# Projection weights of a mixture-of-experts layer: one transfer over 128 rows for each kind instead of two over 64

## The chip, the core and the metric

The kernel runs on one core of a Trainium2 chip. The core has a matrix engine (TensorE: PE for its matmuls, PEld for its weight loads), three engines that work on rows of elements (VectorE or DVE, ScalarE or ACT, GpSimd or POOL), a synchronisation engine SP that here only issues transfers, and 16 DMA engines that carry them between DRAM and the on-chip memory. Each engine runs its own list of instructions in order. An instruction waits on semaphores for what it reads, and what stands behind it on the same engine waits with it. The metric is the time of one execution on the device in microseconds, as a median of several.

## What is computed

The first half is a linear attention with a norm, the second a layer of four experts, each of them a causal attention with its own projections, of which each token uses two:

```python
kv = einsum('bhsd,bhse->bhde', k, v)          # b, h, s, d = 8, 8, 576, 64
out = einsum('bhsd,bhde->bhse', q, kv)
out = out / sqrt(mean(out * out, -1) + 1e-06) * g_norm
x = out.transpose(0, 2, 1, 3).reshape(8, 576, 512)
logits = x @ w_gate                            # 4 experts, the two best are used
for e in range(4):
    q, k, v = x @ wq[e], x @ wk[e], x @ wv[e]  # 512 x 64 each
    a = softmax(causal(q @ k.T / 8))
    y += weight_of_expert(e) * (a @ v @ wo[e])
```

All inputs and the output are float32.

## The kernel before

Each of the eight batches goes through the same steps, and several batches are under way at once. Per batch: load k, v and q (L360 to L379); the products of k and v (`kv`, L382, on TensorE at L387), which are copied out of the accumulator memory as `kvs` (L392) and, with neighbouring rows exchanged, as `kvx` (`kv_move`, L395); 32x32 transposes of q on VectorE (L401); `out_mm` (L408, matmuls at L414), which reads qT, kvs and kvx; copies of its result to `o_sb`; sums of squares and gate logits (L443); a spread of the norm factors over the rows (L562) and the scaled, transposed activations `xT` (L573). Then the experts, two at a time: `proj` (L599, matmuls at L602) makes kT and qT of a pair of experts, `v_mm` (L584, L587) the values of all four; scores (L620), exponentials (L631), masks (L637), the product with the values (L649), scaling (L669), a transposition (L682), and the output product (L694) with its store (L715).

The norm's gain `g_norm` and a constant are folded into the projection weights. Row d of head h in a weight is multiplied by element d of the gain, so a weight is loaded unscaled into a staging area (`lw`, L338) and then copied with the factor into its final tile `w_r` (`ws`, L344). The staging area is the memory of the three tiles `PT`: PT_143 for q, PT_144 for k, PT_145 for v. The final tile `w_r[kind]` has 128 rows (which of two groups of four heads, times 64 elements), four chunks (the head within the group), four experts and 64 columns.

Before, a transfer `lw(kind, eh)` brings two of the four experts in full, 512 rows each, into 64 rows of the staging area: 256 KB as 64 x 16 runs of 256 bytes. A scaling `ws(kind, hh, eh)` takes four heads of two experts out of those 64 rows and writes one half of the rows of `w_r`, all four chunks, for two experts. So one transfer and the two scalings that follow it complete two experts. The projections of batch 0 begin with experts 2 and 3 (pair 1), and experts 0 and 1 (pair 0) follow after `out_mm` of batch 1.

All instructions stand in one list that was written out ahead of time, as three strings: `ORDER` gives the tasks in order, `ENGINE` the engine of each task, `BANKS` the banks of the accumulator memory. A task's instructions go to its engine in the order of that list. A fourth string, `GATE`, limits the loads in flight: the digit n at a load's place makes it wait until the load that is n places earlier in the list of loads has landed (0: no such wait). SP issues the loads in that order, so a load that waits holds back the loads behind it.

Names in rows of the order: k_b_80, v_b_82 and q_b_84 are the buffers of k, v and q of batch 1 (batches use two buffers of each in turn), k_b_79, v_b_81 and q_b_83 those of batches 0 and 2; kvs_86 and kvx_88 are the products of batch 1; xT_133 is the activation of batch 0; kT_136 and qTp_139 are the projections of its pair 1.

Of the kernel before, what the change touches and what calls it, by code (L numbers as in the profile page):

```python
# [24 lines left out]


ORDER = (
    "010A0v0t0D060714130N0P0Q0R050C0U0u0r0s0z020J0S040803000w0x152w0E160I0-"
    "0y0+101112170L1A191C2x180M091E1L1G1H1F2t1D1B1M1N1O0Y0i2u1P1Q1K1R340h2v0W1g1i1I1j1h1J2y2+1k1l0B0d2-"
    "302z31333235362H0e2F0X0f0g0V0c2G372I0b0F383A3B4w393G3H1u1s3C3D2N3E3F4y2O3J1v1S1T1U0O2P1V3K1t1+3L1-"  # L30
    "4x4v513M522Q501X4-"
    "53541W203N4z56574+591w1x583O0Z0a21552J3I3T2K0l0T0m5A0j5E6z6y0k5B5C5G1q1r3P3Q3R1o6x3S3i5F2U1p5H5I1Z3l8+5D1m6+0K"
    "1n3k3j5K3n5J5L3m3U3V5M5N3W1Y5O5P2L1y3X5Q5R5S6-2M8-"
    "3Y1z2R3w3x71735T2T72743Z753a5U782S5l775o3u3b3v5p765V4J4K5k5W5n4H5m90703s42797B3y7A4I8z3+953-"
    "3t229243459693941b1a1c1d970G3z0p7C7GA-"
    "7D9C919A9BB22V99B12W1e1f7E7K7L9D2X98235y5z5w5x7H7I2Y253q3rB30n3d3o9E443p9F7J7F9G249I9M9K622Z63262728290o472A2B"
    "2C2D5s5tB02a2b2cBC4L4M7N9L0q5XD53c3e4R0HBD7O7P7Q5Z407R7S4S2E4W4T7T7U7V416061B7B8B5B6B964657W4N4O9H9J6L6M6J6K7m"
    "D17oD25Y9N9P7p7n9Q7r5u5v7q3f9R9S9T2d2k2l4U2h3gB44648495aBF3h2i4A4C4D4E2e2f5dD39U4F2n2o4B4P4Q4V5+2p679O9ZD47M7X"
    "5-5e6T6UBB6N6O5bBE6R7+7-"
    "4X4Y4Z4a4b4c9V9W4d4e9XBA6S6X5c9Y8L8M5q5r692gBGBH7YBIF8F3BKBO5fBJ5g5hBM6Y2jBN7Z7b8N9p8O9t2m9s7y7z7u6P5i7vD6F682"  # L40
    "8485DH835j6Q2q2r4GDE6VD9BL684f6WDAD87aD79o894jBPF7DB4m9q664g9rDD4h6d6eDG6f7w9+7x6g4n6A2sDCF46Z6a6b4k9-"
    "86878T6E8U4o9w9x6B6C6DF5A0A16cDF6F6G6H6I7dDIDKDM7c7e9a7f9b9cDJDQDO8ABRBSFH8BBQ8VFG7gBTBUBV4iDL7h7i8PDP8W8aBWA6"
    "7j8Q8081A7BbBXBY9u9vDR4p4q7s7t6hA84rA4BZBa8R4sA57k4lA9FCDN8S7l4tFBFAFI9d9e9f9gF9FDFF6u6vBrBvBu8XDT4uBqBs6w6l88"
    "DUDV6m6nBt8G6oDWDX8ZFE6r6s6p6i8C8DFJ8E8HC29hC08I6qDY6j6kC38F8J8Y6t8f8gC19y9z8K9i8hBc8b8c8dBd8iBwBx8eFKFOBeDZFL"
    "FMFSB+B-"
    "FQ8jBfC69jCAADDa9kFTC8DbC7DcC9FR9l9mACANAOCBAPAQDtDwDxDSDdFPDeFNBgBjAVAWAbA2A3AXAY8w8x8yAA8k8lCRCSAcDsDvDuFVFW"
    "FXFYFZFUFaBkABFfATAUARASC4C5AEAFAIFbBhCPCQ9nETCEAG8n8oAJAKAa8mALAHAMFcFdEUAZAdCZFgCaCXCYCVCTAeAfAgAhAi8pAjDfAk"
    "Al8q8rDgDhCdCUE2E3CFCCBiCW8t8uE4E5FeBlBmCcByBzDjFuFw8sE6E7BnBoDyDzAsApFxFvFyDiCe8vFzAtDlAyAzA+ERAvAwAmAnEAAqCb"
    "DkAuESArEVEZCDCGEBAxDnCHBpCICJCKDmEWCLCMCNG4G5EGAoCfCgChCOCjCkEaEfCiD+ClFhG2CmG3EbFiD-EdFjCnFkEXEcFlE8ECEYEDG6"
    "E9GWE0FnGXFoG7GEGFEHEeGCDoDpDqE1G8G9FmFpFqFrDrEEEFGAGBEgGUEIEJG0GDEKELG1GIGVEMENElEOEhEmEnEPEQGeGfGcGdGjGiGHGa"  # L50
    "GbGGEoGYGhEiEjEkEpGJF+F-CuC+C-D0FsFtCvCwCoGZGKGLGMCrGNCsGOGPGgGkGlGQGRCxCtCpCqCyCzGmGnEzE+GoGpGqGrE-"
    "EqEwErEsGSGTGsEtExEyEuF0GtH4H5G+EvF1F2H1H6G-H0H2GuGvGxGwGyGzH3"
)
# [65 lines left out]
def kernel(  # L119
# [125 lines left out]
    def queue(*task):  # L245
        return {"S": nc.sync, "A": nc.scalar, "G": nc.gpsimd}[engine[task]]
# [88 lines left out]
        nc.vector.tensor_reduce(m_b[:], jj[:, :, 2], axis=AX_X, op=add)  # L335
        nc.vector.tensor_scalar(out=m_b[:], in0=m_b[:], scalar1=-1.0, scalar2=None, op0=mult)

    def lw(nm, eh):  # L338
        return queue("lw", nm, eh).dma_start(
            stage[nm][eh * Dh : (eh + 1) * Dh].rearrange("p e h f -> p (e h) f"),  # L340
            w_dram[nm][2 * eh : 2 * eh + 2].rearrange("e (h p) f -> p (e h) f", p=Dh),
        )

    def ws(nm, hh, eh):  # L344
        rows = slice(eh * Dh, (eh + 1) * Dh)
        src = stage[nm][rows, :, 4 * hh : 4 * hh + 4, :]
        dst = w_r[nm][hh * Dh : (hh + 1) * Dh, :, 2 * eh : 2 * eh + 2, :].rearrange("p c e f -> p e c f")
        if engine["ws", nm, hh, eh] == "A":
            nc.scalar.activation(dst, src, ACTF.Copy, scale=g8[rows, 0:1])
        else:  # L350
            ew("ws", nm, hh, eh).tensor_scalar(out=dst, in0=src, scalar1=g8[rows, 0:1], scalar2=None, op0=mult)
# [428 lines left out]
```

## Time and profile before

| | |
|---|---|
| time, median of 3 runs | 208.63 us (208.28 to 209.16) |
| profiled execution, own time | 208.9 us |
| its span in the trace | 206.9 us |
| busy: PE, DVE, ACT, POOL | 185.5, 140.8, 125.9, 77.1 us |
| mean share of the DMA engines, 35 to 41 us | 1.09 |
| projection (L602): matmuls for the key and query weights | 20.6 and 20.8 us in all |
| weight scalings on POOL, 64x512 elements | 1.56, 1.56 and 1.84 us |
| weight scalings on ACT, 64x512 elements | 0.72 us each, six |

The profile shows one execution on the chip. Its views are: a page with the busy time of each engine, the chain of work that ended last, the costliest groups of instructions and the transfers; instructions in order of time (start, duration, engine, line, operation, output from input, and in brackets how long the engine sat idle before and what ended that); busy time by window; and the transfers that were issued in a window, with the time from issue to landing. A "q" behind an engine's name is its instruction queue, so SPq rows are issues of transfers. A clock of 1.00 is the full clock of TensorE. A DMA share above 1 means that packets overlap on the 16 engines.

### The profile page before, as it was taken

What the parts mean: (1) busy time and instruction counts of PE and PEld (TensorE: products, weight loads), DVE (VectorE), ACT (ScalarE), POOL (GpSimd) and SP (SyncE); (2) the same over time, 40 slices, a digit from 0 to 9 for tenths busy, and PEclk for the clock granted to TensorE, in tenths of its full rate; (3) what the DMA queues carried; (4) which work ended last, traced back from release to release, by engine and by line L of the source; (5) the groups of instructions that cost most, each with busy time, mean ns of one, the idle gap of its engine ahead of it and who ended that gap; (6) DMA issues with size and microseconds to landing.
All of it is one profiled execution on the core that took longest, in us unless ns stands there. A gap on an engine that the chain in (4) does not pass through costs nothing.

```text
span 206.9 us, 7270 instructions
## 1 busy us (share of the span) xinstructions
PE 185.5 (90%) x3009; PEld 146.3 (71%) x3020; DVE 140.8 (68%) x359; ACT 125.9 (61%) x216; POOL 77.1 (37%) x187
## 2 busy tenths in 40 slices
...
GB/s 210 361 228 296 268 197 190 367 249 314 351 352 314 329 230 284 49 290 205 219 266 308 277 188 117 97 71 221 37 3 81 82 136 55 205 37 24 159 354 217
DMA packets 41905, 42.62 MB, mean 206 GB/s; under 512 B 17936, under 2 KB 35344, under 8 KB 41872
## 3 DMA queue, kind: packets, MB, share of 16 engines
...
q10 hardware_dynamic: 2208, 1.84, 2.7%
...
## 4 chain that ended last, share of the span: by engine, by line
PE 69%; DMA 10%; DVE 7%; issue 5%; ACT 2%; POOL 2%; DVEq 0%; SPq 0%; POOLq 0%; ACTq 0%
PE ps L602 15%; PE ps L387 8%; PE ps L443 8%; PE ps L587 8%; PE ps L620 8%; PE ps L649 7%; PE ps L414 7%; PE ps L694 7%; DMA k_b<-in_k_dram 6%; DMA OT<-osc 3%; DVE qT L403 2%; DMA q_b<-in_q_dram 2%; DVE kvx L229 2%; PE ps L562 1%; ACT PT L631 1%
## 5 line engine op out<-in xcount | busy, mean ns | idle before, releaser
L631 ACT ACTIVATE PT<-ps 128x1024 bf16<-128x1024 f32 (+1 forms) x64 | 50.7, 837 | 11.7 <-PE ps L620 8.9
L637 POOL TENSOR_SCALAR_AFFINE_SELECT PT<-PT 128x256 bf16<-128x256 bf16 (+1 forms) x80 | 29.2, 389 | 25.2 <-ACT PT L631 24.9
L403 DVE STREAM_TRANSPOSE qT<-q_b 128x576 f32<-128x576 f32 x32 | 23.6, 759 | 13.7 <-DMA q_b<-in_q_dram 11.8
L387 PE MATMUL ps<-v_b,k_b 128*64 128x64 f32 x640 | 22.3, 234 | 6.5 <-DMA k_b<-in_k_dram 5.8
L573 DVE TENSOR_TENSOR xT<-o_sb,ps 128x640 fp32r<-128x640 f32 x30 | 23.4, 814 | 6.3 <-PE ps L562 5.0
L387 PEld LDWEIGHTS ps<-v_b,k_b 128*64 128x64 f32 x640 | 21.4, 149 | 8.5 <-issue 6.2
L587 PE MATMUL ps<-wv_r,xT 128*128 128x256 f32 x160 | 23.6, 289 | 0.4 <-DVE root L474 0.4
L436 POOL TENSOR_TENSOR sq<-o_sb 128x576 f32<-128x576 f32 x16 | 18.4, 1159 | 10.6 <-ACT o_sb L226 7.0
L587 PEld LDWEIGHTS ps<-wv_r,xT 128*128 128x128 f32 x160 | 20.3, 189 | 2.5 <-issue 0.7
L620 PE MATMUL ps<-qTp,kT 64*128 64x64 f32 (+4 forms) x192 | 21.3, 338 | 0.0
L602 PE MATMUL ps<-xT,wq_r 128*128 128x288 f32 x128 | 20.8, 304 | 0.0
L602 PE MATMUL ps<-xT,wk_r 128*128 128x288 f32 x128 | 20.6, 304 | 0.2 <-ACT PT L631 0.2
L602 PEld LDWEIGHTS ps<-xT,wk_r 128*128 128x128 f32 x128 | 17.6, 188 | 2.3 <-issue 0.7
L649 PEld LDWEIGHTS <-PT 128*128 128x128 bf16 x480 | 16.3, 97 | 3.7 <-issue 1.0
L694 PE MATMUL ps<-wo_b,OT 128*128 128x512 bf16 (+1 forms) x85 | 18.1, 344 | 0.8 <-DMA OT<-osc 0.4
L602 PEld LDWEIGHTS ps<-xT,wq_r 128*128 128x128 f32 x128 | 17.6, 188 | 1.3 <-issue 0.4
L649 PE MATMUL ps<-vext,PT 128*128 128x65 bf16 x480 | 18.1, 193 | 0.1
L620 PEld LDWEIGHTS ps<-qTp,kT 64*128 64x128 f32 x192 | 14.0, 185 | 5.3 <-issue 1.4
L669 DVE TENSOR_TENSOR osc<-ps,inv 128x384 bf16<-128x384 f32 (+1 forms) x32 | 15.2, 485 | 2.6 <-POOL inv L665 2.0
L226 ACT COPY o_sb<-ps 128x576 f32<-128x576 f32 x19 | 11.6, 643 | 6.9 <-PE ps L414 6.9
L229 DVE COPY o_sb<-ps 128x576 f32<-128x576 f32 x13 | 9.8, 756 | 8.4 <-PE ps L414 5.6
L414 PE MATMUL ps<-qT,kvs 32*64 32x288 f32 x256 | 13.5, 415 | 1.4 <-issue 0.9
...
## 6 DMA issues: line engine op xcount, KB each, us to landing
...
out_dram<-y SPq DMA_DIRECT2D x24, 256.0 KB, 2.5
...
out_dram<-v_b SPq DMA_DIRECT2D x4, 256.0 KB, 3.6
...
```

Source lines behind the costliest of these rows:

```text
L387: nc.tensor.matmul(p_kv[Dh * t : Dh * t + Dh, j, hh, :], lhsT=kb_[b % NK][:, h, n, :], rhs=vb_[b % NK][:, h, n, :], start=(n == 0), stop=( ...
L403: nc.vector.transpose(qT_[0][:, hh, j * n : (j + 1) * n].rearrange("p j h i -> p (j h i)"), qb_[b % 2][:, hh, j * n : (j + 1) * n, :].rear ...
L414: nc.tensor.matmul(p_o[Dh * hh : Dh * hh + Dh, 0:HALF], lhsT=kvx_[b % 2][rows, hh, :] if m else kvs_[b % 2][rows, g % 2, hh, :], rhs=qT_[0 ...
L436: inst = ew("sq", b, u, p).tensor_tensor(out=dst, in0=src, in1=src, op=mult)
L573: ew("xm", b, u, p).tensor_tensor(out=view(xT_[b % 2]), in0=view(ob_[b % 2]), in1=spread_r.rearrange("p s (m j) -> p m s j", j=32), op=mult)
L587: nc.tensor.matmul(one("v", b, i)[:, n * 256 : (n + 1) * 256], lhsT=xT_[b % 2][:, c, blk * P : (blk + 1) * P], rhs=w_r["v"][:, c].rearrang ...
L602: nc.tensor.matmul(bank_in((nm + "p", b, pr), s)[:, 0:HALF], lhsT=w_r[nm][:, c, 2 * pr : 2 * pr + 2, :].rearrange("p e f -> p (e f)"), rhs ...
L620: nc.tensor.matmul(bank_in(("sc", b, pr, j), el)[:, o : o + hi - lo], lhsT=kT_[(2 * b + pr) % 3][pp, kb * P : (kb + 1) * P], rhs=qTp_[(2 * ...
L631: nc.scalar.activation(PT[:, :, d0 : d0 + o], two("sc", b, pr, j)[:, :, 0:o], ACTF.Exp, scale=scale)
L637: nc.gpsimd.affine_select(out=d, in_=d, compare_op=AluOpType.is_ge, fill=0.0, base=0, pattern=[[0, 2], [1, w]], channel_multiplier=-1)
L649: nc.tensor.matmul(p_O[:, (2 * n + el) * (Hd + 1) : (2 * n + el + 1) * (Hd + 1)], lhsT=PT[:, el, col : col + P], rhs=vx_[b % 2][:, kb, 2 * ...
L694: nc.tensor.matmul(p_y[o * nq : (o + 1) * nq, 0:w], lhsT=OT_[b % 2][:, pr, s0 : s0 + nq], rhs=wo_b[:, pr, o * w : (o + 1) * w], start=(pr ...
```

## The change

A weight's transfer now takes all four experts at once over 128 rows, with row = 64 x (parity of the head) + element, so 512 KB as 128 x 16 runs of 256 bytes. There is one transfer for each of the three kinds in place of two. Since a staging row now holds four heads of one parity for all experts, a scaling `ws(kind, hh, x)` reads two heads of one parity x for four experts, and writes one half of the rows of `w_r`, every second chunk, for all four experts. There are still four scalings of each kind, on the same engines.

```diff
-    out += [("lw", nm, eh) for nm in "qkv" for eh in r2] + [("ws", nm, hh, eh) for nm in "qkv" for eh in r2 for hh in r2]
+    out += [("lw", nm) for nm in "qkv"] + [("ws", nm, hh, x) for nm in "qkv" for x in r2 for hh in r2]
...
-        nm: PT_[n][:].rearrange("p e n -> p (e n)")[:, 0 : 2 * D * E * Hd // P].bitcast(FP32).rearrange("p (e h f) -> p e h f", e=2, h=H)
+        nm: PT_[n][:].rearrange("p e n -> p (e n)")[:, 0 : 2 * D * E * Hd // P].bitcast(FP32).rearrange("p (e n f) -> p e n f", e=E, n=NCH)
...
-    def lw(nm, eh):
-        return queue("lw", nm, eh).dma_start(
-            stage[nm][eh * Dh : (eh + 1) * Dh].rearrange("p e h f -> p (e h) f"),
-            w_dram[nm][2 * eh : 2 * eh + 2].rearrange("e (h p) f -> p (e h) f", p=Dh),
-        )
-
-    def ws(nm, hh, eh):
-        rows = slice(eh * Dh, (eh + 1) * Dh)
-        src = stage[nm][rows, :, 4 * hh : 4 * hh + 4, :]
-        dst = w_r[nm][hh * Dh : (hh + 1) * Dh, :, 2 * eh : 2 * eh + 2, :].rearrange("p c e f -> p e c f")
+    def lw(nm):
+        return queue("lw", nm).dma_start(
+            stage[nm].rearrange("p e n f -> p (e n) f"), w_dram[nm].rearrange("e (n p) f -> p (e n) f", p=P)
+        )
+
+    def ws(nm, hh, x):
+        rows = slice(x * Dh, (x + 1) * Dh)
+        src = stage[nm][rows, :, 2 * hh : 2 * hh + 2, :]
+        dst = w_r[nm][hh * Dh : (hh + 1) * Dh, x : x + 3 : 2, :, :].rearrange("p n e f -> p e n f")
...
-    "000000065544044055564506006553456430300023036240420420606"
+    "000000065544044556450606553456430300023036240420420606"
```

The last pair is `GATE`. Its digits for the dropped loads are gone and most of the others are as before, but they count back in a list that is three entries shorter, so ten of the other loads wait for another load than before. The first v load of batch 2 waited for the last k load of batch 1 and now waits for the k weights. `ORDER` places the k scalings on POOL and ACT and three of the q scalings ahead of the first projection. `BANKS` gives another bank number to 81 of 282 results in the accumulator memory. The line numbers of the changed kernel are one higher from L29 to L338.

On SP, around the loads of batch 1 (`-` before, `+` now):

```order
 L363 DMA k_b_80<-in_k_dram 64x8x320
-L339 DMA PT_144<-in_moe_wk_dram 64x16x64
+L340 DMA PT_144<-in_moe_wk_dram 128x16x64
 L363 DMA v_b_82<-in_v_dram 64x8x320
 L363 DMA k_b_80<-in_k_dram 64x8x256
-L339 DMA PT_143<-in_moe_wq_dram 64x16x64
+L340 DMA PT_143<-in_moe_wq_dram 128x16x64
 L376 DMA q_b_84<-in_q_dram 128x1152
-L339 DMA PT_144<-in_moe_wk_dram 64x16x64
-L339 DMA PT_143<-in_moe_wq_dram 64x16x64
 L363 DMA v_b_81<-in_v_dram 64x8x320
 L363 DMA v_b_81<-in_v_dram 64x8x256
```

The whole k weights stand where their first half stood, ahead of the last v and k loads of batch 1; the whole q weights likewise behind them. The second halves are gone from behind the q load.

On TensorE, the end of `kv` of batch 1 (L387), the first two projections (L602) and the first of `out_mm` of batch 1 (L414), with what each instruction waits for. A name such as Pool_49 is the semaphore that counts POOL's finished instructions, Activation_49 that of ACT. Before:

```order
L387 MATMUL ps<-v_b_82,k_b_80 64x64 x31
L602 MATMUL ps<-xT_133,wk_r 128x288 [waits DVE_49,Pool_49]
L602 MATMUL ps<-xT_133,wk_r 128x288 x3
L602 MATMUL ps<-xT_133,wk_r 128x288 [waits Pool_49]
L602 MATMUL ps<-xT_133,wk_r 128x288 x3
L602 MATMUL ps<-xT_133,wq_r 128x288 [waits Activation_49]
L602 MATMUL ps<-xT_133,wq_r 128x288 x7
L414 MATMUL ps<-qT_89,kvs_86 64x288 [waits DVE_49] x2
```

And with the change:

```order
L387 MATMUL ps<-v_b_82,k_b_80 64x64 x31
L602 MATMUL ps<-xT_133,wk_r 128x288 [waits DVE_49,Activation_49,Pool_49]
L602 MATMUL ps<-xT_133,wk_r 128x288 x7
L602 MATMUL ps<-xT_133,wq_r 128x288 [waits DVE_49,Pool_49]
L602 MATMUL ps<-xT_133,wq_r 128x288
L602 MATMUL ps<-xT_133,wq_r 128x288 [waits Activation_49]
L602 MATMUL ps<-xT_133,wq_r 128x288 x5
L414 MATMUL ps<-qT_89,kvs_86 64x288 [waits DVE_49]
```

The order of the matmuls is the same. The first key projection now waits for ACT too, and the first query projection for DVE and POOL as well as ACT.

On POOL, around the copies to kvx of batch 1. Before:

```order
L573 TENSOR_TENSOR xT_133<-o_sb_90,sq_92 128x10x64 x2
L284 MEMSET o_sb_91 128x4x64
L228 COPY kvx_88<-kvs_86 32x128 x4
L351 TENSOR_SCALAR wk_r<-PT_144,g_64 64x2x4x64
L351 TENSOR_SCALAR wq_r<-PT_143,g_64 64x2x4x64
L292 MEMSET PT_143 128x2x64
L436 TENSOR_TENSOR sq_92<-o_sb_91 128x2x288
```

And with the change:

```order
L573 TENSOR_TENSOR xT_133<-o_sb_90,sq_92 128x10x64 x2
L285 MEMSET o_sb_91 128x4x64
L229 COPY kvx_88<-kvs_86 32x128 x4
L351 TENSOR_SCALAR wk_r<-PT_144,g_64 64x4x2x64
L351 TENSOR_SCALAR wq_r<-PT_143,g_64 64x4x2x64
L293 MEMSET PT_143 128x2x64
L436 TENSOR_TENSOR sq_92<-o_sb_91 128x2x288
```

Nothing moved here: both scalings stand behind the four copies as before, with the new form. On ACT the k scaling that stood behind a q scaling, after the copy to kvs of batch 1, now stands ahead of it, and on DVE the q scaling stands ahead of the last transpose of q of batch 1 instead of behind the copy to kT.

More of the change, by code (lines that the diff above doesn't have):

```diff
@@ L34 @@
[L34 to L50, printed above, removed]
@@ new lines @@
+    "1j6x0K1k3h3g5H3k5G5I3j3R3S5J5K3T1V5L5M2I1v3U5N5O5P6y2J8y3V1w2O3t3u6+705Q2Q6-"
+    "713W723X5R752P5i745l3r3Y3s5m735S4G4H5h5T5k4E5j8z6z3p3-76783v774F8w3x923y3q1-8-"
+    "40429390911Y1X1Z1a940G3w0m797DAy7A998+9798A-"
+    "2S96A+2T1b1c7B7H7I9A2U95205v5w5t5u7E7F2V223n3oB00k3a3l9B413m9C7G7C9D219F9J9H5-"
+    "2W60232425260l442728292A5p5qAz2X2Y2ZB94I4J7K9I0n5UD23Z3b4O0HBA7L7M7N5W3z7O7P4P2B4T4Q7Q7R7S3+5z5+B4B5B2B3B66162"
+    "7T4K4L9E9G6I6J6G6H7jC+7lC-"
+    "5V9K9M7m7k9N7o5r5s7n3c9O9P9Q2a2h2i4R2e3dB14345465XBC3e2f47494A4B2b2c5aD09R4C2k2l484M4N4S5x2m649L9WD17J7U5y5b6Q"
@@ new lines @@
+    "6RB86K6L5YBB6O7x7y4U4V4W4X4Y4Z9S9T4a4b9UB76P6U5Z9V8I8J5n5o662dBDBE7VBFF5F0BHBL5cBG5d5eBJ6V2gBK7W7Y8K9m8L9q2j9p"
+    "7v7w7r6M5f7sD3F37-"
+    "8182DE805g6N2n2o4DDB6SD6BI654c6TD7D57XD49l864gBMF4D84j9n634d9oDA4e6a6bDD6c7t9x7u6d4k672pD9F16W6X6Y4h9y83848Q6B"
+    "8R4l9t9u68696AF29z9+6ZDC6C6D6E6F7aDFDHDJ7Z7b9X7c9Y9ZDGDNDL87BOBPFE88BN8SFD7dBQBRBS4fDI7e7f8MDM8T8XBTA37g8N7z7+"
+    "A4BYBUBV9r9sDO4m4n7p7q6eA54oA1BWBX8O4pA27h4iA6F9DK8P7i4qF8F7FF9a9b9c9dF6FAFC6r6sBoBsBr8UDQ4rBnBp6t6i85DRDS6j6k"
+    "Bq8D6lDTDU8WFB6o6p6m6f898AFG8B8EB-"
@@ new lines @@
+    "9eBz8F6nDV6g6hC08C8G8V6q8c8dB+9v9w8H9f8eBZ8Y8Z8aBa8fBtBu8bFHFLBbDWFIFJFPBxByFN8gBcC39gC7AADX9hFQC5DYC4DZC6FO9i"
+    "9jA9AKALC8AMANDqDtDuDPDaFMDbFKBdBgASATAY9-"
+    "A0AUAV8t8u8vA78h8iCOCPAZDpDsDrFSFTFUFVFWFRFXBhA8FcAQARAOAPC1C2ABACAFFYBeCMCN9kEQCBAD8k8lAGAHAX8jAIAEAJFZFaERAW"
+    "AaCWFdCXCUCVCSCQAbAcAdAeAf8mAgDcAhAi8n8oDdDeCaCRD-"
+    "E0CCC9BfCT8q8rE1E2FbBiBjCZBvBwDgFrFt8pE3E4BkBlDvDwApAmFuFsFvDfCb8sFwAqDiAvAwAxEOAsAtAjAkE7AnCYDhArEPAoESEWCACD"
+    "E8AuDkCEBmCFCGCHDjETCICJCKG1G2EDAlCcCdCeCLCgChEXEcCfDxCiFeF-CjG0EYFfDyEaFgCkFhEUEZFiE5E9EVEAG3E6GTDzFkGUFlG4GB"
@@ new lines @@
+    "VVVVVVVAVGVVGPPVVVVPAPAPAPAPAPAPAPAPAGGGGPVGVPVVVSPAPAPAPAPAPAGGGGPVGVPVGVSPASPASPVSPVSPVSSSSSSSPPPPAGGVVVVPPV"
+    "AAAAAVGPPAAVVVVVVVVVVVVVVVVAVVVVVPPVVVVPAPAPAPAPAPAPAPAPAGGGGPVVVPVVVSPAPVPAPAPAPAGGGGPVGVPVGVSPASPASPASPVSPAS"
+    "SSSSSSPPPPAAGVVVVPPAGAGAAAAPPAAGVVGVVVVVGVVVVVVAVVVVVPPVVVVPVPAPVPAPAPAPAPAPAGGGGPVVVPVVVSPVPVPAPAPAPAGGGGPVGV"
+    "PVGVSPVSPASPVSPASPVSSSSSSSPPPPVVGVVVVPPVAAGVGAGPPAAVVVAVGVVVVVVVVVVAVVVVGPPVVVVPVPAPAPAPAPAPAPAPAGGGGPVGVPVGVS"
+    "PVPAPAPAPAPAGGGGPVGVPVVVSPVSPASPASPVSPASSSSSSSPPPPAAGVVVVPPAAAGVAAGPPAAVVVGVGVVVGVVVVVGAVGVVVPPVVVVPAPAPAPAPAP"
@@ L71 @@
+    "45672045672345106714502345671024567301346701235467501423670145234502367450123450142367230154234250123102310230"
     "12"
```

41 lines of the change are left out of this document (17 added, 24 removed).

## The prediction

> **What bounds the kernel now.** I read the page's head first, then the chain of work that ended last, then busy time by window where that chain leaves TensorE, and then the order of time there.
>
> ```profile
> span 206.9 us, 7270 instructions
> PE 185.5 (90%) x3009; PEld 146.3 (71%) x3020; DVE 140.8 (68%) x359; ACT 125.9 (61%) x216; POOL 77.1 (37%) x187
> PE 69%; DMA 10%; DVE 7%; issue 5%; ACT 2%; POOL 2%; DVEq 0%; SPq 0%; POOLq 0%; ACTq 0%
> ```
>
> TensorE is busy for 90% of the span and makes 69% of the chain: it is the bound, in the order in which its work is written. Its idle 21.4 us (206.9 - 185.5) lie mostly near the start, and the largest piece is the one beside the edit. The columns of the next view are a window's sum, then busy time and instructions of PE, PEld, DVE, ACT and POOL, then granted clock, DMA share, GB/s.
>
> ```profile
> 23.00:25.00 2.00, 0.34 (x12) 0.10 (x4) 0.94 (x3) 0.92 (x2) 0.00 (x0) 1.00 1.17 286
> 25.00:27.00 2.00, 0.00 (x0) 0.00 (x0) 1.81 (x3) 1.08 (x2) 1.43 (x1) 0.92 1.21 173
> 27.00:29.00 2.00, 0.00 (x0) 0.00 (x0) 0.00 (x0) 0.00 (x0) 1.85 (x3) 0.50 1.10 246
> 29.00:31.00 2.00, 1.88 (x36) 1.91 (x38) 0.00 (x0) 0.42 (x1) 0.00 (x0) 0.50 1.23 167
> 31.00:33.00 2.00, 2.00 (x43) 2.00 (x42) 0.59 (x1) 0.30 (x1) 0.00 (x0) 0.50 0.31 49
> 33.00:35.00 2.00, 2.00 (x22) 1.72 (x20) 0.90 (x3) 1.27 (x3) 0.73 (x3) 0.87 0.85 208
> 35.00:41.00 6.00, 6.00 (x92) 4.74 (x92) 4.36 (x7) 4.29 (x7) 4.85 (x6) 1.00 1.09 368
> ```
>
> From 23.3 to 29.1 TensorE does nothing while the DMA engines are full. The clock falls to one half at about 26.7 (a mean of 0.92 over 25 to 27 is 0.32 us of half clock) and is back at about 33.5 (0.87 over 33 to 35). In order of time:
>
> ```profile
> 17.64 1.85 SPq L363 DMA_DIRECT2D k_b<-in_k_dram  x1
> 29.12 4.52 PE L387 MATMUL ps<-v_b,k_b 128*64 128x64 f32 x80 [5.78 <-DMA k_b<-in_k_dram]
> 33.57 1.33 PE L602 MATMUL ps<-xT,wk_r 128*128 128x288 f32 x8
> 33.68 0.37 ACT L226 COPY kvs<-ps 128x256 f32<-128x256 f32 x1 [2.38 <-PE ps L387]
> 34.18 1.29 POOL L228 COPY kvx<-kvs 32x128 f32<-32x128 f32 x4 [5.33 <-ACT kvs L226]
> 34.82 0.72 ACT L349 ACTIVATE wk_r<-PT,g 64x512 fp32r<-64x512 f32 x1
> 34.85 1.32 PE L602 MATMUL ps<-xT,wq_r 128*128 128x288 f32 x8
> 35.58 1.56 POOL L351 TENSOR_SCALAR wk_r<-PT,g 64x512 fp32r<-64x512 f32 x1
> 35.62 0.92 DVE L351 TENSOR_SCALAR wq_r<-PT,g 64x512 fp32r<-64x512 f32 x1
> 36.10 0.74 PE L414 MATMUL ps<-qT,kvs 32*64 32x288 f32 x16
> 37.23 1.56 POOL L351 TENSOR_SCALAR wq_r<-PT,g 64x512 fp32r<-64x512 f32 x1
> ```
>
> L387 is kv of batch 1, which waits for the last half of k (issued at 17.64). Right behind it, at 33.57 and 34.85, run the first two projections (batch 0, experts 2 and 3). POOL writes the weight parts of L351 only at 35.58 and 37.23, when those projections have started: today they do not need them, since one transfer holds two experts in full and its two scalings complete them.
>
> **The change, part by part.** Call T the end of kv of batch 1 (33.64: 29.12 + 4.52).
>
> *The wait that is added.* A scaling now writes half of the rows and two of the four chunks, for all four experts. A projection for two experts reads all rows and all chunks, so it needs all four scalings of its kind. For k they are two on ACT, one on DVE and one on POOL; the order of POOL shows its part still behind the four copies of kvx, and those follow ACT's copy of kvs, which follows kv itself. So POOL runs as today, counted from T: kvx ends at T + 1.83 (34.18 + 1.29), the k part at T + 3.50 (35.58 + 1.56), the q part at T + 5.15 (37.23 + 1.56). The first projection starts at T + 3.6 instead of at once and ends at T + 4.9; the q projection waits for T + 5.15, some 0.1 us more for the signal, and takes 1.25 (34.85 to 36.10). The output matmuls of batch 1 (L414) thus start at T + 6.5, where they started at T + 2.46 (36.10). That is **+4.0 us**. Behind the waiting projections TensorE holds everything else, so nothing of its own fills the gap, and DVE, ACT and the batch 0 scores wait behind it. ACT's k part (34.82, 0.72 long) and DVE's q part (0.92) are early enough to hide under POOL; without POOL's chain the step would be priced by ACT's k part alone, which ends near T + 1.2 (kvs at T + 0.41, then 0.72).
>
> The scaling reads 4x2x64 elements where it read 2x4x64, a form no row shows. Nearest below is POOL's 1.56; above, its v part:
>
> ```profile
> 47.69 1.84 POOL L351 TENSOR_SCALAR wv_r<-PT,g 64x512 fp32r<-64x512 f32 x1 [0.42 <-DMA PT<-in_moe_wv_dram]
> ```
>
> That bounds the two POOL operations between 0 and +0.6 us together, and below zero by about as much, as in 35.58 to 37 DVE ran beside POOL and will now mostly be idle. I keep 1.56.
>
> *The transfer that grows.* The k weights come as 512 KB ahead of the last halves of v and k of batch 1; so far 256 KB stood there and the rest came behind. Each run of a row stays 256 B, so packets double there. What 256 KB more cost:
>
> ```profile
> 24.43 1.10 SPq L339 DMA_DIRECT2D PT<-in_moe_wk_dram  x1
> 27.21 1.38 SPq L339 DMA_DIRECT2D PT<-in_moe_wq_dram  x1
> PT<-in_moe_wk_dram SPq DMA_DIRECT2D x1, 256.0 KB, 9.0
> PT<-in_moe_wq_dram SPq DMA_DIRECT2D x1, 256.0 KB, 7.5
> DMA packets 1191, 0.33 MB, mean 167 GB/s; under 512 B 1183, under 2 KB 1183, under 8 KB 1191
> ```
>
> Two such transfers one behind the other landed at 33.4 (24.43 + 9.0) and 34.7 (27.21 + 7.5): 1.3 us apart. The last row is the window 29 to 31, almost only such packets: 1183 in 2 us, so 1024 take 1.7 us. At the other end, if 128 rows move as fast as 64 did, nothing is added. I take 1.3 (0 to 1.7), the distance of two landings. Kv then starts at 30.4. Of the delay the clock returns a part: it rises at 33.5 whatever kv does, and the same work costs
>
> ```profile
> 42.84 2.55 PE L387 MATMUL ps<-v_b,k_b 128*64 128x64 f32 x80
> ```
>
> 2.55 at full clock. Today 4.38 us at half clock (29.12 to 33.5) did all but 0.14 us of it, a rate of 0.55. From 30.4 half clock does 1.7, 0.86 are left, and T is 34.4: **+0.7 us** (0 to +1.0; +1.4 if the rise at 33.5 fails and 4.52 is paid in full from 30.4).
>
> The q weights, also whole, are behind that k transfer. Their first half landed at 30.6 (22.09 + 8.5):
>
> ```profile
> PT<-in_moe_wq_dram SPq DMA_DIRECT2D x1, 256.0 KB, 8.5
> ```
>
> Two steps of 1.3 bring it to 33.2; ACT's first q part then ends at 33.9, before T and the kvs copy behind it on ACT. With 1.7 twice it ends 0.3 us past T, the end I keep for the range. The q load of batch 1 that DVE transposes lands under 3 us later than at 32.4, and DVE still finishes its q part ahead of POOL's.
>
> *What is removed.* Three issues on SP, where 24.43 and 27.21 stand. The limits on loads in flight now count to other loads: the first v load of batch 2 waits for the k weights instead of for k of batch 1 and leaves near 26 instead of
>
> ```profile
> 29.09 3.74 SPq L363 DMA_DIRECT2D v_b<-in_v_dram  x2
> ```
>
> So the hole in the DMA engines (share 0.31 from 31 to 33) fills, and batch 2's loads come up to 1.7 us earlier (0.69 of 2 us, and 0.15 of the next 2). After 41, though, the stalls that TensorE shows with a length of 0.45 us and more are these, and none up to 90 ends with a load:
>
> ```profile
> 49.31 0.48 PE L414 MATMUL ps<-qT,kvs 32*64 32x288 f32 x5 [0.94 <-issue]
> 62.09 0.32 PE L562 MATMUL ps<-rc,esel 32*128 32x160 bf16 x8 [0.45 <-ACT kvs L226]
> 78.91 0.49 PE L414 MATMUL ps<-qT,kvx 32*64 32x288 f32 x6 [1.00 <-DVE kvx L229]
> ```
>
> They sum to 2.4 us. A later TensorE can take back at most about that; since they end with ACT and DVE work that itself hangs on TensorE, I take 0.5 (0 to 2.4). The new bank numbers of the products' results change who must be read out first at some places; no row prices that, and I let it lie in the range with 0.5 either way.
>
> *The sum.* 4.0 + 0.7 - 0.5 = +4.2 us. The profiled execution took 208.9 (span 206.9 and 2.0 around it), 0.3 above the median of 208.63; 4.2 on the median is **212.8**.
>
> **The rivals.**
>
> *The clock falls again.* TensorE has only about 1 us of work from 33.5 to 38, then a projection, a short wait, a projection. The trace shows one fall after a gap of 5.8, with 0.34 us of work in the 3.7 us before 26.7. If the new gap of 3.5 us also brings half clock, the work behind it runs at 0.55 for one stretch like today's, or half of one: of 6.8 us some 1.5 to 3.1 are lost, 214.3 to 215.9. Against: the gap is 2.3 us shorter than the one seen. The Trainium skill, "TensorE: Matmul & The Clock Gate", section "HAM oscillation — how this bites in real kernels", warns of idle gaps over about 3.4 us, which speaks against this change; the trace agrees for its 5.8 us gap and has none of 3.5 us. By that rule the forecast would lie at this rival, and it gets its chance from the lengths above. Chance 0.17.
>
> *More is taken back.* The merged transfer moves as fast as a half did (+0 instead of +0.7), and the stalls above give back up to 2.4: 4.0 - 2.4 = +1.6, 210.2, to +3.3, 211.9. Chance 0.15.
>
> *The loads pace the middle, and the kernel gets faster.* The DMA engines are full from 35 to 41 (share 1.09). If the batches behind are paced by landings and TensorE's busy time hides it, the delay is absorbed in full and the 1.7 us by which loads are earlier remain: 206.9. It decides if kv of batches 2 and 3 start when their loads land. Against: no stall there ends with a load. The Trainium skill, "DMA: Bandwidth & Descriptors", section "Rules for kernel authors", advises one transfer over 128 partitions in place of two over disjoint halves, as the halves share the same engines; that is for the change, and the two landings 1.3 us apart agree that halves run in turn. Chance 0.04.
>
> *It does not matter.* The projections do not really wait, or all 4.7 us are absorbed without a gain: 208.6. The changed order shows that the first projection newly waits for ACT beside POOL and DVE, and the program could not be right without; so only absorption is left. Chance 0.04.
>
> **How the numbers follow.** Forecast 0.60, clock 0.17, more taken back 0.15, faster 0.04, no change 0.04. The forecast's own bounds are 212.8 with -1.3 and +1.5. From both sides the range leaves out the two last rivals and the far end of the clock's: 210.3 to 215.6. Half a per cent, 1.0 us, is about what a measurement of this kernel can tell from none. Slower by more: 0.60 + 0.17 + 0.15 = 0.92.
>
> **What would show it.** Right: TensorE idle for about 3.5 us between kv of batch 1 and the first L602, ended by POOL's L351 on wk_r, and a second wait of some 0.3 us ended by wq_r; kv's start near 30.4; L414 of batch 1 near 41 instead of 36.1; every later group shifted by an equal 4 to 5 us. Wrong: the first L602 right behind L387, POOL's L351 ahead of kvx, kv starting before 29.1, a half clock after 35, or the shift shrinking from batch to batch by stalls that vanish.

## The result: 211.24 us against 209.31 us, and the profile after

The kernel with the change took 211.24 us, the median of 20 runs (210.34 to 213.1); the kernel before, beside it, 209.31 us (206.53 to 213.03). The ratio is 1.0142 with a 95% interval of 1.0113 to 1.0171, so the change costs 2.4 to 3.6 us on 209.31. Ratios here and below compare fast executions only (one that is over 1.5% above the fastest of its kernel is left out), so a ratio can differ from that of the two medians. The forecast was 4.2 us more, 212.8 us on the median shown then.

The head of the page of the kernel after: span, busy times, and the shares of the chain of work that ended last.

```profile
span 208.8 us, 7259 instructions
PE 185.6 (89%) x3009; PEld 147.1 (70%) x3020; DVE 140.4 (67%) x359; ACT 125.9 (60%) x216; POOL 77.0 (37%) x187
PE 70%; DVE 11%; DMA 5%; issue 5%; POOL 3%; ACT 2%; SPq 1%; POOLq 0%; DVEq 0%; ACTq 0%
```

TensorE does the same work as before (185.6 us against 185.5), and the span grew by 1.9 us: the difference is idle time. In the chain DMA fell from 10% to 5%, while POOL rose from 2% to 3% and DVE from 7% to 11%. In order of time around the edit, kernel after:

```profile
16.94 3.01 SPq L363 DMA_DIRECT2D v_b<-in_v_dram  x1
27.55 4.48 PE L387 MATMUL ps<-v_b,k_b 128*64 128x64 f32 x80 [4.26 <-DMA k_b<-in_k_dram]
32.07 0.37 ACT L227 COPY kvs<-ps 128x256 f32<-128x256 f32 x1 [1.84 <-PE ps L387]
32.47 0.72 ACT L349 ACTIVATE wk_r<-PT,g 64x512 fp32r<-64x512 f32 x1
32.57 1.27 POOL L229 COPY kvx<-kvs 32x128 f32<-32x128 f32 x4 [5.51 <-ACT kvs L227]
33.95 1.56 POOL L351 TENSOR_SCALAR wk_r<-PT,g 64x512 fp32r<-64x512 f32 x1
35.56 2.29 PE L602 MATMUL ps<-xT,wk_r 128*128 128x288 f32 x8 [3.52 <-POOL wk_r L351]
35.59 1.56 POOL L351 TENSOR_SCALAR wq_r<-PT,g 64x512 fp32r<-64x512 f32 x1
37.65 1.70 PE L602 MATMUL ps<-xT,wq_r 128*128 128x288 f32 x8
39.27 0.74 PE L414 MATMUL ps<-qT,kvs 32*64 32x288 f32 x16
```

The brackets tell the story. Kv of batch 1 starts at 27.55 instead of 29.12, and so ends earlier (T = 32.03 instead of 33.64). Behind it TensorE now stands idle for 3.52 us until POOL has written its part of `wk_r`, at 33.95 + 1.56 = 35.51. Then both projections run slowly, 2.29 and 1.70 us where the rows of before show 1.33 and 1.32. The windows of the same execution say why (the column ahead of the last two is the granted clock, the next the DMA share):

```profile
27.00:29.00 2.00, 1.45 (x27) 1.48 (x29) 0.00 (x0) 0.00 (x0) 0.07 (x1) 0.50 0.61 134
29.00:31.00 2.00, 2.00 (x43) 2.00 (x42) 0.05 (x1) 0.72 (x1) 0.00 (x0) 0.50 0.93 352
31.00:33.00 2.00, 1.03 (x21) 0.89 (x18) 1.77 (x3) 0.90 (x2) 0.39 (x2) 0.79 0.90 261
33.00:35.00 2.00, 0.00 (x0) 0.00 (x0) 0.00 (x0) 0.90 (x2) 1.81 (x4) 1.00 1.08 371
35.00:37.00 2.00, 1.44 (x6) 1.44 (x7) 0.00 (x0) 0.00 (x0) 1.91 (x2) 0.56 1.11 372
37.00:39.00 2.00, 2.00 (x11) 2.00 (x11) 0.76 (x1) 0.00 (x0) 0.36 (x2) 0.58 1.04 407
39.00:41.00 2.00, 2.00 (x59) 1.43 (x65) 0.30 (x1) 1.10 (x2) 0.00 (x0) 1.00 1.12 322
```

The clock comes back near 32, then falls a second time: 0.56 and 0.58 are 1.76 and 1.68 us of half clock, 3.4 us in all, where the kernel before has 1.00 from 35 on. In the gap from 33 to 35 POOL is busy for 1.81 us, ACT for 0.90 and DVE not at all. The hole in the DMA engines from 31 to 33 is gone (0.90 instead of 0.31).

How long the second fall lasts differs between executions. In a second profile of the same kernel (r2_after; the wait there is 3.56 us) the same columns are:

```profile
33.00:35.00 2.00, 0.00 (x0) 0.00 (x0) 0.30 (x1) 0.78 (x2) 1.81 (x4) 0.87 1.05 343
35.00:37.00 2.00, 1.53 (x6) 1.53 (x7) 0.00 (x0) 0.00 (x0) 1.91 (x2) 0.50 1.01 333
37.00:39.00 2.00, 2.00 (x11) 2.00 (x10) 0.76 (x1) 0.00 (x0) 0.27 (x2) 0.50 1.06 412
39.00:41.00 2.00, 2.00 (x27) 1.20 (x34) 0.00 (x0) 0.64 (x1) 0.00 (x0) 0.50 1.09 343
41.00:43.00 2.00, 2.00 (x51) 1.24 (x36) 1.03 (x2) 1.22 (x2) 0.30 (x1) 0.92 0.83 159
```

That is 6.8 us of half clock (0.52 + 3 x 2.00 + 0.32), and it reaches past both projections into the output matmuls.

Follow the shift. The output matmuls of batch 1 start 3.17 us later (39.27 against 36.10), kv of batch 2 starts 3.16 later, and the last matmuls of the program end 2.39 us later (199.87 + 2.99 against 197.49 + 2.98). In the rows below, after:

```profile
46.00 2.55 PE L387 MATMUL ps<-v_b,k_b 128*64 128x64 f32 x80
199.87 2.99 PE L694 MATMUL ps<-wo_b,OT 128*128 128x512 bf16 x17
```

and before:

```profile
197.49 2.98 PE L694 MATMUL ps<-wo_b,OT 128*128 128x512 bf16 x17
```

So the loss has one place, at kv and the projections behind it. Behind it the shift changes by single stalls. The 0.94 us stall of before at 49.31, which ended with "issue", has no row here, and at 53.26 against 51.47 the shift is 1.79. A new stall, after, takes it up to 2.67 (60.51 against 57.84):

```profile
60.51 1.32 PE L602 MATMUL ps<-xT,wk_r 128*128 128x288 f32 x8 [0.86 <-DVE root L474]
```

The second profiles of the two kernels (r1_before and r2_after) have a shift of 3.04 at kv of batch 2 and of 2.94 at the end, and r1_before has no such stall near 49. So 0.8 us came back in one pair of profiles and 0.1 in the other.

### The profile page after: what moved, and what is told of

The parts are those of the page before. It is cut to its first block, busy times and chain, and to the rows that moved or that the text cites. A ratio compares the mean times of both kernels' runs of the same rounds, so it can differ in the third digit from the quotient of the medians.

```text
span 208.8 us, 7259 instructions
## 1 busy us (share of the span) xinstructions
PE 185.6 (89%) x3009; PEld 147.1 (70%) x3020; DVE 140.4 (67%) x359; ACT 125.9 (60%) x216; POOL 77.0 (37%) x187
## 4 chain that ended last, share of the span: by engine, by line
PE 70%; DVE 11%; DMA 5%; issue 5%; POOL 3%; ACT 2%; SPq 1%; POOLq 0%; DVEq 0%; ACTq 0%
PE ps L602 15%; PE ps L587 8%; PE ps L387 8%; PE ps L620 7%; PE ps L443 7%; PE ps L414 7%; PE ps L649 7%; PE ps L694 7%; DMA k_b<-in_k_dram 4%; DVE qT L403 3%; DMA q_b<-in_q_dram 2%; DVE kvx L230 2%; PE ps L562 2%; SPq L363 1%; DVE part L485 1%
## 5 line engine op out<-in xcount | busy, mean ns | idle before, releaser
L387 PE MATMUL ps<-v_b,k_b 128*64 128x64 f32 x640 | 22.3, 234 | 5.7 <-DMA k_b<-in_k_dram 4.3
L387 PEld LDWEIGHTS ps<-v_b,k_b 128*64 128x64 f32 x640 | 21.4, 149 | 7.7 <-issue 5.1
L602 PE MATMUL ps<-xT,wk_r 128*128 128x288 f32 x128 | 21.5, 314 | 4.6 <-POOL wk_r L351 3.5
L602 PEld LDWEIGHTS ps<-xT,wk_r 128*128 128x128 f32 x128 | 18.4, 197 | 6.8 <-POOL wk_r L351 3.7
L602 PE MATMUL ps<-xT,wq_r 128*128 128x288 f32 x128 | 21.2, 309 | 0.0
L602 PEld LDWEIGHTS ps<-xT,wq_r 128*128 128x128 f32 x128 | 18.3, 194 | 1.1 <-issue 0.4
L665 POOL TENSOR_TENSOR inv<-inv,g_gate 128x4 f32<-128x4 f32 (+1 forms) x16 | 3.3, 205 | 30.0 <-DVE inv L661 29.8
```

The source lines that it names most:

```text
L387: nc.tensor.matmul(p_kv[Dh * t : Dh * t + Dh, j, hh, :], lhsT=kb_[b % NK][:, h, n, :], rhs=vb_[b % NK][:, h, n, :], start=(n == 0), stop=( ...
L602: nc.tensor.matmul(bank_in((nm + "p", b, pr), s)[:, 0:HALF], lhsT=w_r[nm][:, c, 2 * pr : 2 * pr + 2, :].rearrange("p e f -> p (e f)"), rhs ...
```

## The experiments

Two claims were to be tested: that the wait behind POOL is the whole loss, and, since kv came earlier and not later, that the new transfer is a gain. Two rivals to the second claim came with the change: the shifted limits on loads (`GATE`) and the new banks. Ratios are to the kernel before, run beside each.

| run | what it is | median us | ratio (95%) |
|---|---|---|---|
| e1_early | change, four scalings earlier | 206.72 | 0.9874 (0.9804 to 0.9944) |
| e3_wait_alone | before, with the wait added | 211.26 | 1.0116 (1.0059 to 1.0173) |
| e4_two_halves | change, transfers split into 64 rows | 213.79 | 1.0254 (1.0206 to 1.0302) |
| e5_fill_gap | change, zero matmuls in the gap | 211.04 | 1.013 (1.008 to 1.018) |
| e6_early_halves | e1_early, transfers split | 207.74 | 0.9938 (0.9883 to 0.9992) |
| e7_gates | e1_early, loads held as before | 205.31 | 0.9804 (0.9741 to 0.9867) |
| e8_banks | e1_early, banks of before | 204.65 | 0.9791 (0.9728 to 0.9854) |
| e9_fill_kv | e1_early, zero matmuls ahead of kv | 205.88 | 0.983 (0.9768 to 0.9892) |
| e10_all | the last three together | 205.93 | 0.983 (0.9782 to 0.9878) |

### The wait taken away

POOL's two scalings go ahead of the copies to kvx, and two of ACT's ahead of its copy to kvs. The order of the two engines:

```diff
 L285 MEMSET o_sb_91 128x4x64
-L229 COPY kvx_88<-kvs_86 32x128 x4
 L351 TENSOR_SCALAR wk_r<-PT_144,g_64 64x4x2x64
 L351 TENSOR_SCALAR wq_r<-PT_143,g_64 64x4x2x64
+L229 COPY kvx_88<-kvs_86 32x128 x4
...
-L349 ACTIVATE wq_r<-PT_143,g_64 64x4x2x64
+L349 ACTIVATE wk_r<-PT_144,g_64 64x4x2x64
+L349 ACTIVATE wq_r<-PT_143,g_64 64x4x2x64 x2
 L227 COPY kvs_86<-ps 128x256
-L349 ACTIVATE wk_r<-PT_144,g_64 64x4x2x64
-L349 ACTIVATE wq_r<-PT_143,g_64 64x4x2x64
```

> The changed kernel with four scalings moved: on POOL the k and q parts ahead of the four copies to kvx of batch 1, on ACT the k and the second q part ahead of the copy to kvs. Theory A (the added wait behind POOL is the loss, and the second stretch of half clock hangs on it): the 3.5 us stall of TensorE ahead of the first projection is gone, the two projections take 2.6 us together instead of 3.8, out_mm of batch 1 starts near 34.6 with kv at 27.5, and the time falls by 2 to 4.5 us against the change's 211.2, to 206.7 to 209.2, so not above the kernel before. Theory B (the loss lies elsewhere, in bank numbers or in the transfers, and the stall would be absorbed): the stall goes, but the time stays within 1 us of 211.2.

206.72 us, 4.5 below the kernel after and below the kernel before too. A second profile of the same kernel (r3_e1) shows the order of time:

```profile
27.30 4.53 PE L387 MATMUL ps<-v_b,k_b 128*64 128x64 f32 x80 [4.04 <-DMA k_b<-in_k_dram]
27.48 1.56 POOL L351 TENSOR_SCALAR wk_r<-PT,g 64x512 fp32r<-64x512 f32 x1
31.76 1.77 PE L602 MATMUL ps<-xT,wk_r 128*128 128x288 f32 x8
32.30 1.28 POOL L229 COPY kvx<-kvs 32x128 f32<-32x128 f32 x4 [1.27 <-ACT kvs L227]
33.37 1.22 PE L602 MATMUL ps<-xT,wq_r 128*128 128x288 f32 x8
34.52 0.74 PE L414 MATMUL ps<-qT,kvs 32*64 32x288 f32 x16
```

POOL's scaling runs under kv; the projection at 31.76 follows kv without a bracket, that is, without idle time. (In the first profile kv starts later, at 29.82, and the projection follows it without idle time as well.) The wait, with the fall of the clock that it brings, is the loss, and with it gone the rest of the change is a gain.

### The wait put into the kernel before

The 64-row transfers stay. POOL takes over a part of the second halves of the k and q scalings, which the first projections read, and DVE and ACT take what POOL did.

```diff
 ws-k, heads 0-3, experts 2,3:  DVE  -> POOL, ahead of the first projection, behind the copies to kvx
 ws-q, heads 4-7, experts 2,3:  ACT  -> POOL, likewise
 ws-k, heads 0-3, experts 0,1:  POOL -> DVE
 ws-q, heads 4-7, experts 0,1:  POOL -> ACT
```

> The kernel before, transfers and order of TensorE unchanged, with only the engines of four scalings exchanged: POOL, behind its copies to kvx of batch 1, now makes the k and q parts that the first two projections need, and DVE and ACT those that POOL made. Theory A: TensorE stalls 3.4 to 3.6 us ahead of the first projection and the time rises by 2.5 to 5 us over the kernel before. Theory B: the stall shows in the trace but the time rises by under 1 us.

Its trace shows the stall at the same place:

```profile
27.44 4.12 PE L387 MATMUL ps<-v_b,k_b 128*64 128x64 f32 x80 [4.45 <-DMA k_b<-in_k_dram]
33.47 1.61 POOL L351 TENSOR_SCALAR wk_r<-PT,g 64x512 fp32r<-64x512 f32 x1
35.13 2.29 PE L602 MATMUL ps<-xT,wk_r 128*128 128x288 f32 x8 [3.58 <-POOL wk_r L351]
39.27 1.26 PE L414 MATMUL ps<-qT,kvs 32*64 32x288 f32 x16
```

3.58 us, ended by POOL. The time, though, rose by 2.1 us of the medians (1.2 to 3.6 by the interval), under most of what was expected and under the 4.5 that e1_early got back. The profiled execution took 214.18 us, 2.9 above the median, so only the order is read from it. The mechanism stands; why its price is lower here stays open.

### The transfer split again

```diff
-        return queue("lw", nm).dma_start(stage[nm] ..., w_dram[nm] ...)
+        for x in range(2):
+            rows = slice(x * Dh, (x + 1) * Dh)
+            inst = queue("lw", nm).dma_start(stage[nm][rows] ..., w_dram[nm] ...[rows])
+        return inst
```

> The changed kernel with each weight's transfer cut in two of 64 rows, issued one behind the other; layout, order and scalings stay. Theory R (the 64-row form is slow because fewer rows are written at once, and the 128-row form gains it back): the median 256 B packet of the k weights takes near 28 ns as before instead of 18, the k weights land later by 1.5 us or more after their issue, kv of batch 1 starts 1 to 3 us later than with one transfer, near 29 to 30.5, and the time rises by 0.5 to 2 us. Theory C (the early kv of the changed kernel is chance): kv starts where it did within 0.5 us, packets take 18 ns, time within 0.5 us of the changed kernel.

> The kernel of e1_early (scalings early, no stall) with each weight's transfer cut in two of 64 rows. Theory R (the 128-row form is what makes e1_early faster than the kernel before): 256 B packets take near 30 ns at the median, kv of batch 1 starts later in relation to the issues ahead of it, and the time rises by 1.5 to 3 us over e1_early's 206.7, to 208.2 to 209.7, the kernel before. Theory G (e1_early gains by the new limits on loads in flight and the new banks): within 0.7 us of e1_early.

With the wait, 213.79 us: 2.5 more than the kernel after, above the 0.5 to 2 that was expected, and the intervals (from 1.0206, up to 1.0171) do not meet. Without it, 207.74: 1.0 more than e1_early, between the two theories, and there the intervals overlap. How fast the runs of 256 bytes go can be read from windows that hold almost nothing else; the first line is packets in 2 us, the second the share of the 16 engines. After, from 18 to 20:

```profile
DMA packets 1710, 0.52 MB, mean 262 GB/s; under 512 B 1621, under 2 KB 1710, under 8 KB 1710
q1 hardware_dynamic: 1710, 0.52, 121.0%
```

e4_two_halves, from 19 to 21:

```profile
DMA packets 1087, 0.28 MB, mean 142 GB/s; under 512 B 1078, under 2 KB 1087, under 8 KB 1087
q1 hardware_dynamic: 1087, 0.28, 132.9%
```

In both windows the engines are full. A packet took 1.21 x 16 x 2 us / 1710 = 23 ns on average over 128 rows, and 1.329 x 16 x 2 us / 1087 = 39 ns over 64. The window of before that the prediction quoted has 1191 packets at 122.8%, 33 ns. The traces scatter: other such windows with over 1000 packets give 22 to 26 ns with one transfer (after, e1_early, r3_e1, e8_banks) and 29 to 39 with halves (before, r1_before, e4, e6). So the form of the transfer matters; the same bytes in two halves are slower. The split also costs three more issues on SP, which these runs do not separate.

### The gap filled, and the start of kv filled

`ZEROS` lists tasks ahead of which TensorE multiplies zeros into the bank that the task then fills anew. Nothing of the computation is left out.

```diff
-ZEROS = {('kv', 0, 0, 1): 9}
+ZEROS = {('kv', 0, 0, 1): 9, ('kp', 0, 1): 4}
```

> The changed kernel with four matmuls of zeros written ahead of the first projection, into its bank, about 3.4 us of work in the 3.5 us stall; nothing else moves. Theory K (half clock behind the stall costs): the granted clock is full from about 32.2 on, the two projections take 2.6 us together instead of 3.8, out_mm starts 1 to 1.3 us earlier in relation to the end of kv, and the time falls by 0.7 to 1.3 us against the changed kernel. Theory L (the clock's second fall is absorbed later): the projections get faster but the time stays within 0.4 us.

The clock stays up, and the projections take their full-clock time:

```profile
30.47 3.71 PE L734 MATMUL ps<-zeros 128*128 128x512 f32 x8
34.10 1.33 PE L602 MATMUL ps<-xT,wk_r 128*128 128x288 f32 x8
35.75 1.32 PE L602 MATMUL ps<-xT,wq_r 128*128 128x288 f32 x8 [0.32 <-POOL wq_r L351]
37.01 0.74 PE L414 MATMUL ps<-qT,kvs 32*64 32x288 f32 x16
49.59 0.32 PE L443 MATMUL ps<-o_sb,wg 128*32 128x160 f32 x1 [1.33 <-issue]
```

The four are eight rows of the trace. Here kv ended at 30.54, so `out_mm` starts at T + 6.47, where after it is T + 7.24: the second fall of the clock cost 0.77 us there. For the next projection, which starts at T + 8.59 here (39.13), it is 0.78 in after (41.40, T + 9.37) and 2.0 in r2_after:

```profile
42.53 1.32 PE L602 MATMUL ps<-xT,wk_r 128*128 128x288 f32 x8
```

(T there is 31.91, so this is T + 10.62.) Yet the time is that of the kernel after, so at the end of the program no price of the clock is shown. In the one trace of e5 a stall of 1.33 us ended by "issue", for which the profile names no cause, takes away about half of the lead over after (2.26 us at `out_mm`), and the rest is gone by 119 us.

In e9_fill_kv the same four stand ahead of kv of batch 1, on top of e1_early.

> The kernel of e1_early with four matmuls of zeros ahead of kv of batch 1, into its bank, while its loads are on the way. If the half clock over kv costs what the rows say (4.2 to 4.5 us for work that takes 2.55), kv takes 2.5 to 2.9 us, and the time falls by 1 to 1.8 us against e1_early, to 204.9 to 205.7. If the early landing of kv's loads is held up by the zeros, or the gain is absorbed as with the filled stall of e5_fill_gap: within 0.5 us of e1_early.

Kv then takes 2.55 us instead of 4.5, and the time is 0.8 below e1_early, inside the intervals and between what the two theories said. The zeros also held kv back: its last load had landed at 26.45 (20.15 + 6.3).

```profile
23.79 3.71 PE L734 MATMUL ps<-zeros 128*128 128x512 f32 x8 [1.27 <-DVE xT L573]
27.43 2.55 PE L387 MATMUL ps<-v_b,k_b 128*64 128x64 f32 x80
```

### Limits on loads, banks, and all together

e7_gates makes each load wait for the same load as before; e8_banks puts the string of bank numbers of before into e1_early.

```diff
-    "000000065544044556450606553456430300023036240420420606"
+    "000000065544044334560605443456430300023036240420420606"
```

> The kernel of e1_early with the limits on loads in flight set so that each load waits for the same load as in the kernel before (the first v load of batch 2 again for the last k load of batch 1). Theory G: the hole in the DMA engines near 31 to 33 us comes back and the time rises by 1 to 2.5 us over e1_early. Theory R: within 0.7 us of e1_early, since TensorE waits for no load behind kv of batch 1.

> The kernel of e1_early with the bank numbers of the kernel before. Theory that banks do not matter: within 0.5 us of e1_early. Rival (the new banks carry a part of the gain, or cost): off by more than 0.7 us either way.

> The scalings early as in e1_early, with the limits on loads of before (as in e7_gates), the banks of before (as in e8_banks) and four zero matmuls ahead of kv of batch 1 (as in e9_fill_kv). What is left of the change is then the form of the transfer and the scalings. Against e1_early's 206.72 the three alone gave 205.31, 204.65 and 205.88, differences of 1.4, 2.1 and 0.8 us whose intervals overlap. If each is a gain of its own (theory S) the sum is 4.3 us: about 202.4, a ratio near 0.967. If they are scatter about one program (theory C), whose kv of batch 1 starts at 26.4 to 29.8 us as loads happen to land, only the banks or the fill may stay: 204 to 206, a ratio of 0.975 to 0.985. In both the trace shows no wait between kv of batch 1 and the projections of over 0.4 us, kv of batch 1 about 1.5 us ahead of 29.12 and at full clock.

Neither is slower than e1_early, so neither the shifted limits nor the new banks carry its gain over before. Both are faster by more (1.4 and 2.1 us) than the 0.7 us that was allowed for no difference, but the intervals overlap, and the differences do not add: all three edits together gave 205.93, where the sum of the three differences would be 202.4. That fits scatter about one program, with a ratio of 0.979 to 0.987; a small cost of the new banks is not excluded. In e10's trace the zero matmuls held kv back further (its last load had landed at 28.0, 20.70 + 7.3), as the clock was at one half when they began and they took 5.34 us instead of 3.71. In order of time:

```profile
24.46 5.34 PE L734 MATMUL ps<-zeros 128*128 128x512 f32 x8 [0.97 <-ACT sq L581]
29.73 2.55 PE L387 MATMUL ps<-v_b,k_b 128*64 128x64 f32 x80
```

and the window in which they began (granted clock 0.50):

```profile
25.00:27.00 2.00, 2.00 (x3) 0.68 (x2) 0.97 (x2) 0.72 (x2) 2.00 (x2) 0.50 1.23 285
```

### Three more profiles, and all of them in two numbers

> The kernel before once more, for a second profile. If the start of kv of batch 1 is a matter of the transfer's form, it lies 11.5 to 12.5 us behind the issue of the second v load of batch 1 as in the first profile; if it scatters from run to run by as much as the forms differ, anywhere from 10 to 12.5.

> The changed kernel once more. By the transfer's form kv of batch 1 starts 10 to 11 us behind the issue of the second v load of batch 1; by scatter anywhere from 10 to 12.5. The stall ahead of the first projection is 3.4 to 3.6 us in either case.

> The kernel of e1_early once more. TensorE goes from kv of batch 1 to the first projection without a stall, and the granted clock does not fall behind kv. Kv starts 10 to 11 us behind the issue of the second v load of batch 1 by the transfer's form, 10 to 12.5 by scatter.

They took 209.66, 211.8 and 207.64 us, one execution each, in the order of the medians. Two numbers split every trace: where kv of batch 1 starts, and how long from there to the end of the last matmul. Since kv waits for the last v and k loads of its batch, its start is given also from the issue of the second v load (16.94 after). In e4 and e6 the profile names "issue" and not a load as what ended kv's wait; with the filler of e9 and e10 kv starts behind the zeros, so they are left out.

| trace | kv starts | from issue of the v load | kv start to last matmul |
|---|---|---|---|
| before; r1_before | 29.12; 30.21 | 12.14; 12.38 | 171.35; 170.66 |
| e6_early_halves | 28.86 | 11.48 | 171.61 |
| e1_early; r3_e1 | 29.82; 27.30 | 11.88; 10.40 | 170.48; 171.14 |
| e7_gates; e8_banks | 27.45; 27.08 | 10.30; 10.43 | 169.82; 170.45 |
| after; r2_after | 27.55; 27.97 | 10.61; 10.56 | 175.31; 175.85 |
| e5_fill_gap | 26.44 | 9.97 | 176.44 |
| e4_two_halves | 29.41 | 12.10 | 176.16 |
| e3_wait_alone | 27.44 | 10.80 | 178.58 |

The last column has two groups: 169.8 to 171.6 without the wait, 175.3 and more with it. The wait costs about 5 us in the kernels with the change (means of 170.8 and 175.9), in e5 with the clock held up too. The 178.58 of e3 is left aside, as only the order is read from that profile. The column before it follows the form of the transfer, less sharply: 9.97 to 11.88 for one transfer over 128 rows (median 10.43), 10.80 to 12.38 for two over 64 (median 12.10). So about 1.7 us are gained ahead of kv, and after loses 4.8 against e1_early's two traces behind it: together +3, as the ratio has it.

## Why the prediction was right in sign and too high

**The wait that is added: right.** It was to be idle time of 3.5 us ended by POOL's part of `wk_r`; it is 3.52. POOL was to end that part at T + 3.50; it ended at T + 3.48. The q projection and `out_mm` at T + 6.5: with the clock held up (e5) 6.47. The new form of the scaling takes 1.56 us like the old one, so its bounds were not needed. e1_early shows the cause by removing it.

**The transfer that grows: wrong in sign.** This is the step that failed. The prediction took 1.3 us for 256 KB more ahead of the last halves of v and k, from two landings of 64-row transfers 1.3 us apart, had kv start at 30.4, and counted +0.7. Kv started at 27.55, 1.6 us earlier than before and not 1.3 later. Its "other end", that 128 rows move as fast as 64 did and nothing is added, was not far enough: a packet took 22 to 26 ns instead of 29 to 39, and all of the k weights landed 8.5 us after their issue at 13.77, where half of them had taken 10.3 from 13.78:

```profile
PT<-in_moe_wk_dram SPq DMA_DIRECT2D x1, 512.0 KB, 8.5
```

In all nine traces with one transfer the 512 KB take 8.5 to 9.2 us; the first 256 KB take 10.3 in both profiles of before and 8.9 in e3. That the k weights, landed earlier, then leave the DMA engines to kv's own loads is argued from this, not shown. The times of the two landings were rightly read, but they price the old form only; they are also landings of two kinds of weights in the same 64 rows, so they do not bear on whether halves run in turn. The sentence of the Trainium skill, "DMA: Bandwidth & Descriptors", section "Rules for kernel authors", against two transfers to disjoint halves of the partitions agrees with e4 (2.5 us lost by the split); e6's 1.0 points the same way, inside its interval. In these runs the packets of the halves were also slower in themselves.

Two smaller points of the same step: T for a kv that starts at 30.4 and pays 4.52 in full is 1.3 us later, not 1.4; and the clock does not rise at 33.5 whatever kv does, but at about 32 in after and 31 in r2_after, where kv started earlier, and at 35.6 in r1_before, where kv started at 30.21 and took 4.53.

**The clock falls again: it did.** The prediction left it to a rival at 0.17 and 1.5 to 3.1 us, because the new gap was shorter than the one seen. The gap of 3.52 us was enough, as by the rule of the Trainium skill, "TensorE: Matmul & The Clock Gate", section "HAM oscillation — how this bites in real kernels", that the prediction cites, which warns of gaps over about 3.4 us. In after the half clock lasted 3.4 us and cost 7.24 - 6.47 = 0.77 us ahead of `out_mm`, half of the rival's lower end, as it fell on two projections of which the second waits for POOL's q part anyway. In r2_after it lasted 6.8 us and cost 2.0, inside the rival's range; e3 and e4 also have 6.8.

**What is taken back: 0.8 and 0.1 for 0.5.** In the first pair of profiles the shift shrinks from 3.16 at kv of batch 2 to 2.39, in the second from 3.04 to 2.94. The rival in which loads pace the middle did not happen: in after kv of batches 2 and 3 waits for no load, and every later batch is late by 2 to 3 us.

The sum from the first pair of profiles: -1.6 for the transfer, +4.0 for the wait, +0.8 for the clock, -0.8 taken back, +2.4 at the last matmul. From the second: -2.8, +3.8, +2.0 and -0.1, which is +2.9. The errors of the forecast, in the first pair -2.3 on the transfer, +0.8 on the clock and -0.3 on what is taken back, left it 1.2 to 2.3 us too high.

That 211.24 lies in the stated range is thus in part luck, as the error on the transfer and the one on the clock have opposite signs. The time also lies in the band of the rival in which more is taken back (210.2 to 211.9), whose first condition, a merged transfer that adds nothing, was more than met. And three of the prediction's own signs of being wrong came: kv started before 29.1, there is half clock after 35, and in the first pair the shift shrinks as a stall vanishes.

What stays open: the transfer's 1.7 us rest on medians of seven and five traces that overlap; e6, split and without the wait, is still faster than before (0.9938), which the form of the transfer cannot explain; the clock's price does not show in the time of e5; and e3's wait cost less in time than in its trace.
